# Three parts of a row table, a register load and a gather at other places of an expert stage

## The chip, the cores and the metric

The kernel runs on one core of a Trainium2 chip. The metric is the device time of one execution in microseconds (us): the median of the runs, beside one execution taken with the profiler. The engines are named as the profile names them: PE is TensorE, PEld its weight load, DVE VectorE, ACT ScalarE, POOL GpSimd, SP the engine that issues most DMAs. A name with a q (DVEq) is that engine's sequencer.

## What is computed

Three layers in a row: sigmoid attention, a mixture of experts in which each token goes to the one expert of its largest logit, and a gated feed-forward layer. Cut to its core:

```python
scores = q @ k.T / sqrt(64) - log(448)          # 4 batches, 12 heads, 448 tokens
x = sigmoid(scores) @ v                         # -> 1792 tokens x 768
xn, en = x / norm(x), expert_emb / norm(expert_emb)
logits = xn @ en.T / tau                        # 8 experts
idx, gate = argmax(logits), max(softmax(logits))
for e in range(8):
    m = idx == e
    out[m] = gate[m] * (relu(x[m] @ w1[e]) @ w2[e])   # 768 -> 1024 -> 768
y = (sigmoid(out @ w_gate) * (out @ w_val)) @ w_out   # 768 -> 1536 -> 768
```

All of it is float32; matrix products that need the precision are made as three products of a rounded part `hi` and a rest `lo`.

## The kernel before

**The expert stage.** Tokens are sorted by expert into tiles of 128 rows. `NSTAT` = 14 tiles are always computed, numbered p = 0 to 13; tiles past that are computed only if the data need them, in the body of an `If` (`tail_tiles`, line 1236; the branch is put down to line 1238), and with these data its body is skipped. Experts that leave only a few rows over get these rows in quarter tiles, the small tokens.

For each tile p: `gather(p)` fetches the rows from `xd` in DRAM by an indirect DMA that POOL issues; `front(p)` turns them on TensorE, ScalarE casts the result to `xh` (hi), and VectorE makes `xl` (lo) of it; four `h_chunk(p, c)` multiply by w1, ScalarE applies relu; `turn(p)` turns that and makes `hh` on ScalarE and `hl` on VectorE; four `y_chunk(p, c)` multiply by w2; `y_scale(p)` and `y_out(p)` scale by the gate and store the rows, by the row table `ridx`, to `yd`. The h chunks of tile p alternate with the y chunks of tile p - 1.

**Weights.** Each chunk of weights is loaded by SP into a raw buffer. `split_next()` makes the next chunk's `hi` on ScalarE (line 280) and its `lo` on VectorE (line 281) in a ring of four, and then issues the load that takes over the raw buffer. One `split_next()` follows each chunk of matmuls, so the splits of the w1 of tile 3 stand behind the h chunks of tile 2, and those of the w2 of tile 2 behind the h chunks of tile 3.

**Order.** The schedule is written out by hand: each engine works off its instructions in the order of the program, and semaphores hold an instruction until its inputs are there and its buffer is free. PSUM tiles come from `slot(...)`, four buffers taken in turn. Counted from there, `y_chunk(2, 0)` takes the buffer that the body of the `If` uses.

**The steps that the change touches.**
- `gate_b`, `gate_exp`, `gate_c`, `gate_d` make the gate weights; `gate_exp` is one exponential on ScalarE (line 873), for which a table is loaded; `gate_c` ends with products on POOL, `gate_d` has the small matmuls `psg` and ends with `gate_s` on VectorE (line 894).
- `turn(1)` (line 1773) is the turn of tile 1, called behind `gate_exp()`.
- `table_rows` (line 818) makes on VectorE the table of rows at which results are stored (`ridx`, `rowq`), and `rowb`. It is called once, behind the h chunks of tile 2 (line 1862).
- `n_tiles` (line 1869) loads the number of tiles from SBUF into a register of every engine; the `If` compares it.
- `front(3, later)` (line 1808) puts the making of `xl` of tile 3 off until behind the last h chunk of tile 2. `xl` has one buffer for all tiles.
- `small_ids` and `gather_small` (lines 811, 1159) make the list `idq` of the small tokens on VectorE and fetch their rows; `front_small` turns them on TensorE behind `turn(3)`.

```python
1808                front(3, later)
1811                later.pop()()
1813                turn(2)
1814                small_ids()
1815                gather_small()
1862            table_rows()
1869            n_tiles = nc.values_load(tabs["n"], min_val=0, max_val=NPAIR)
1870            tail_tiles(NSTAT)
```

Of the kernel before, what the change touches and what calls it, by code (L numbers as in the profile page):

```python
# [11 lines left out]
F32R = mybir.dt.float32r  # L12
# [10 lines left out]
D = H * HD  # L23
# [3 lines left out]
P = 128  # L27
# [10 lines left out]
NPAIR = N // P + E - 1  # L38
# [11 lines left out]
NW1 = KD * F1 // CH  # L50
# [99 lines left out]
def routed_kernel(ctx: ExitStack, tc: tile.TileContext, kqP, vP, emb, tau, w1P, w2P, wffP, cst, out):  # L150
    nc = tc.nc
# [53 lines left out]
    tabs = {}  # L205
# [609 lines left out]
        RED(out=rs, in_=r, axis=AX.X, op=ALU.add)  # L815
        V.tensor_copy(idq, rs)

    def table_rows():

        STT(out=tn, in0=tabs["ef"], scalar=-16.0, in1=tn, op0=ALU.mult, op1=ALU.add)  # L820
        have = per_tile(tabs["tot"], "rh")
        kept = per_tile(tabs["some"], "rs")
        for v in (have, kept):
            STT(out=v, in0=tn, scalar=float(-P), in1=v, op0=ALU.mult, op1=ALU.add)
            TT(out=v, in0=v, in1=once, op=ALU.mult)

        i = PAD
        for a, b in runs:
            TS(out=sums[:, 0, i : i + b - a], in0=kept[:, a:b], scalar1=0.0, scalar2=float(P), op0=ALU.max, op1=ALU.min)
            i += b - a  # L830
        for n, d in enumerate((1, 2, 4, 8, 16)):
            x = sums[:, n % 2]
            TT(out=sums[:, 1 - n % 2, PAD:], in0=x[:, PAD:], in1=x[:, PAD - d : PAD + NCOL - d], op=ALU.add)
        base = R("rb", [P, NCOL])
        i = PAD
        for a, b in runs:
            V.tensor_scalar_add(base[:, a:b], sums[:, 1, i - 1 : i - 1 + b - a], float(-N))
            i += b - a
        STT(out=rowb, in0=tn, scalar=float(-P), in1=base, op0=ALU.mult, op1=ALU.add)
        STT(out=rowb, in0=have, scalar=0.0, in1=rowb, op0=ALU.is_gt, op1=ALU.mult)  # L840
        big, few = slice(0, NPAIR), slice(NPAIR, NCOL)
        pt = [C("part").to_broadcast([P, NPAIR]), C("tq").to_broadcast([P, NQ])]
        for k, w in enumerate((big, few)):
            TT(out=have[:, w], in0=have[:, w], in1=pt[k], op=ALU.is_gt)
        TT(out=base, in0=base, in1=have, op=ALU.mult)
        V.tensor_scalar_add(base, base, float(N))
        ridx = cpool.tile([P, NPAIR], I32, name="ridx")
        rowq = cpool.tile([P, NQ], I32, name="rowq")
        for k, w in enumerate((big, few)):
            TT(out=base[:, w], in0=base[:, w], in1=pt[k], op=ALU.add)  # L850
        TT(out=base, in0=base, in1=own_row, op=ALU.subtract)
        TT(out=base, in0=base, in1=moves, op=ALU.mult)
        TT(out=base, in0=base, in1=own_row, op=ALU.add)
        V.tensor_copy(ridx, base[:, big])
        STT(out=rowq, in0=base[:, few], scalar=4.0, in1=C("jq").to_broadcast([P, NQ]), op0=ALU.mult, op1=ALU.add)
        tabs["r"], tabs["rq"] = ridx, rowq
# [11 lines left out]
    def gate_b():  # L868
        norm(ss, root, R("nt", [CP, NT]))
        TT(out=sh, in0=sh, in1=bc3(ss, E), op=ALU.mult)  # L870

    def gate_exp():
        A.activation(sh, sh, AF.Exp)
# [62 lines left out]
    def front(p, later=None):  # L936
        xg = xg_t.pop(p)
        ps = slot(f"xTp{p}")
        psf = ps.rearrange("p a b -> p (a b)")
        for k in range(KD):  # L940
            T.transpose(psf[:, k * P : (k + 1) * P], xg[:, k * P : (k + 1) * P], ident)  # L941
        if 0 <= p - 1 - PA < NA or p == PZ + 3:
            turn_small(min(p - 1 - PA, NA), psf[:, D : D + 256])
        hi = xp.tile([P, D], F32R, tag="xh", name=f"xh{p}")
        lo = xp.tile([P, D], F32R, tag="xl", name=f"xl{p}", bufs=1)
        A.copy(hi, psf[:, :D])
        xg_t["T", p] = (hi, lo)
        rest = lambda: V.tensor_sub(lo, psf[:, :D], hi)  # L948
        if later is None:
            rest()  # L950
        else:
            later.append(rest)
# [816 lines left out]
    gather(3)  # L1769
    y_chunk(0, 2, part[2])  # L1770
    gate_b()
    gate_exp()
    turn(1)
    y_chunk(0, 3, part[3])
    gate_c()
    for c in range(NW2):
        y_chunk(1, c, part[c])
        if c == 1:
            front(2)
            gate_d()  # L1780
            y_scale(0)
        split_next()
    own_rows()
    y_scale(1)
# [2 lines left out]
    for p in range(2, NSTAT):  # L1787
# [17 lines left out]
        for c in range(NW1):  # L1805
            h_chunk(p, c)
            if p == 2 and c == NW1 - 2:
                front(3, later)
                gather(5)
            elif p == 2 and c == NW1 - 1:  # L1810
                later.pop()()
            elif p == 3 and c == 0:
                turn(2)
                small_ids()
                gather_small()
            split_next()
            if c == 1 and p - PZ in (0, 1, 3):
                small_step((0, 2, 0, 6)[p - PZ])
            y = {(NSTAT - 2, 0): "T2", (NSTAT - 2, 2): "T4"}.get((p, c))
# [39 lines left out]
                    decode(DEC_ORDER[DEC_ATT + k], 2)  # L1859
            y_out(p - 1)  # L1860
        else:
            table_rows()
            y_out(0)
            y_out(1)
            tail = [buf("tail0", SB_Y, 6, 512, dt=F32R), buf("tail1", (SB_Y, 6 * 512), 4, 512, dt=F32R)]
            tail += [dp.tile([P, 6, 512], F32, tag="w64", name="tail_w"),
                     dp.tile([P, CH], F32, tag="w32", name="tail_x"), slot("tail")]
            tc.mark_branch_hint_location("beyond", hint='LikelyTaken', engines=[mybir.EngineType.PE])
            n_tiles = nc.values_load(tabs["n"], min_val=0, max_val=NPAIR)
            tail_tiles(NSTAT)  # L1870
        if 2 < p < NSTAT - 1:
            turn(p)
# [69 lines left out]
```

## Time and profile before

| | |
|---|---|
| median of three runs | 962.5 us (962.39 to 963.03) |
| the profiled execution | 966.3 us, of which 964.2 are the span from its first to its last instruction |
| TensorE busy | 932.3 us, 97% of the span |
| VectorE, ScalarE, POOL busy | 737.5, 544.6, 146.8 us |
| attention | 0 to about 157 us |
| expert stage | about 157 to 475 us; tiles 1 to 3, around which the change lies, 169 to 251 |
| feed-forward | about 475 us to the end |

A timeline gives the instructions of one engine in order, equal ones merged; the bracket behind one is the idle time of the engine before it and what released it. The windows give for each stretch how long an engine was busy and the share of full speed at which TensorE's clock was granted (1.00 is 2.4 GHz, 0.50 is 1.2 GHz). The times are those of the profiled execution.

### The profile page before, as it was taken

The page shows a single profiled execution, that of the slowest core. Times are in us where ns is not written, and L with a number is a line of the kernel's source. Part 1 is how long each engine was busy: PE and PEld are TensorE (multiplying, and loading weights), DVE is VectorE, ACT ScalarE, POOL GpSimd, SP SyncE. Part 2 cuts the span into 40 slices and gives each one's busy share as a digit, 9 for nine tenths or more (in the row PEclk, how much of TensorE's full clock was granted, in tenths as well). Part 3 has the DMA queues.
Part 4 walks back from the last instruction along what each step waited for, and adds up shares of the span by engine and source line. Part 5 has one row for each costly group of instructions (what it writes and reads, how often), then busy time and mean ns, then how long its engine had stood idle before and what let it go on. Part 6 is the DMA issues. An engine that isn't in the chain of part 4 may idle for free.

```text
span 964.2 us, 14875 instructions
## 1 busy us (share of the span) xinstructions
PE 932.3 (97%) x5757; PEld 784.3 (81%) x5757; DVE 737.5 (76%) x912; ACT 544.6 (56%) x645; POOL 146.8 (15%) x124
## 2 busy tenths in 40 slices
PE   9999999997999999999899999999998999999998
PEld 4555555886887788888788999989997999999998
DVE  6867767888899776799858888776896666658674
ACT  6586776575676676778644334446655434335551
POOL 0011113232062222224400000000220000000011
PEclk9999999998999999999889999999999999999999
DMA  8999867454699989766404564255131122125112
GB/s 306 334 327 344 319 215 267 163 167 155 259 401 417 345 323 334 261 262 201 148 1 163 196 196 164 82 203 206 66 132 44 55 66 66 66 99 197 50 50 82
DMA packets 36974, 186.40 MB, mean 193 GB/s; under 512 B 4680, under 2 KB 6744, under 8 KB 32800
## 3 DMA queue, kind: packets, MB, share of 16 engines
q1 hardware_dynamic: 25680, 134.29, 39.4%
q0 software_dynamic: 11216, 51.09, 14.1%
q8 instruction: 46, 0.75, 0.3%
q14 instruction: 32, 0.26, 0.1%
HBM read 180.94 MB, written 35.88 MB: 225 GB/s over the span
## 4 chain that ended last, share of the span: by engine, by line
PE 68%; DVE 3%; ACT 2%; DMA 2%; issue 1%; ACTq 0%; DVEq 0%; POOLq 0%
PE pb L1415 15%; PE pb L1414 15%; PE pb L1416 15%; PE h L1095 9%; PE y L1079 3%; PE y L1081 3%; PE y L1080 3%; PE qh L1184 2%; PE qy L1207 2%; DMA Y<-xd,idq 1%; PE hTp L1114 1%; DMA Y<-yd 1%; DVE rg L281 1%; PE xTp L941 1%; DVE tl L1577 1%
## 5 line engine op out<-in xcount | busy, mean ns | idle before, releaser
L281 DVE TENSOR_TENSOR rg<-raw,rg 128x1536 fp32r<-128x1536 f32 x104 | 180.2, 1757 | 36.9 <-ACT rg L280 32.6
L280 ACT CAST rg<-raw 128x1536 fp32r<-128x1536 f32 x102 | 150.2, 1480 | 64.8 <-PE y L1080 31.3
L1415 PE MATMUL pb<-yl,wh 128*128 128x448 f32 x288 | 106.8, 371 | 2.2 <-DVE yl L1350 2.2
L1095 PE MATMUL h<-rg,xh 128*128 128x512 f32 x336 | 103.6, 403 | 0.3 <-ACT rg L280 0.3
L1416 PE MATMUL pb<-th,sr 128*128 128x384 f32 x294 | 98.4, 335 | 1.4 <-DVE sr L1616 1.4
L1414 PE MATMUL pb<-th,sr 128*128 128x384 f32 x294 | 98.9, 337 | 0.0
L1415 PE MATMUL pb<-tl,sr 128*128 128x384 f32 x294 | 98.4, 335 | 0.2 <-DVE tl L1577 0.2
L436 ACT ACTIVATE attn<-sc,bias_s 128x896 f32<-128x896 f32 x84 | 79.2, 1003 | 28.6 <-PE sc L434 28.2
L1409 DVE TENSOR_TENSOR wl<-wr,wh 128x1536 fp32r<-128x1536 f32 (+1 forms) x43 | 68.0, 1581 | 17.9 <-ACT wh L1404 15.6
L1095 PEld LDWEIGHTS h<-rg,xh 128*128 128x128 f32 x336 | 62.0, 190 | 15.2 <-issue 1.6
L448 PE MATMUL av<-attn,v 128*64 128x448 f32 (+1 forms) x384 | 70.6, 545 | 0.3 <-DVE xT L453 0.2
L1079 PE MATMUL y<-rg,hh 128*128 128x384 f32 x192 | 67.5, 351 | 3.4 <-DVEq L1238 3.4
L1404 ACT CAST wh<-wr 128x1536 fp32r<-128x1536 f32 (+1 forms) x43 | 57.3, 1332 | 18.5 <-PE pb L1415 14.3
L1080 PE MATMUL y<-rg,hl 128*128 128x384 f32 x192 | 65.7, 342 | 1.4 <-DVE hl L1120 1.4
L1081 PE MATMUL y<-rg,hh 128*128 128x384 f32 x192 | 65.5, 341 | 1.5 <-DVE rg L281 1.5
L1095 PE MATMUL h<-rg,xl 128*128 128x512 f32 x168 | 61.9, 396 | 0.9 <-DVE xl L948 0.9
L1415 PEld LDWEIGHTS pb<-yl,wh 128*128 128x128 f32 x288 | 54.8, 190 | 7.3 <-DVE yl L1350 3.0
L1643 POOL DMA_INDIRECT out<-o,idc x12 | 17.5, 1460 | 271.5 <-ACT o L1661 227.6
L1416 PEld LDWEIGHTS pb<-th,sr 128*128 128x128 f32 x294 | 55.2, 188 | 1.7 <-DVE sr L1616 1.7
L1415 PEld LDWEIGHTS pb<-tl,sr 128*128 128x128 f32 x294 | 55.2, 188 | 0.6 <-DVE tl L1577 0.6
L1414 PEld LDWEIGHTS pb<-th,sr 128*128 128x128 f32 x294 | 55.2, 188 | 0.0
L1614 ACT CAST sr<-G 128x768 fp32r<-128x768 f32 x42 | 35.1, 839 | 30.4 <-PE pb L1415 18.5
(499 smaller groups left out, 2109.5 us busy)
## 6 DMA issues: line engine op xcount, KB each, us to landing
raw<-in_w1P SPq DMA_DIRECT2D x52, 768.0 KB
raw<-in_w2P SPq DMA_DIRECT2D x52, 768.0 KB
q<-wob SPq DMA_DIRECT2D x14, 1152.0 KB
wr<-wd SPq DMA_DIRECT2D x19, 768.0 KB
sg<-in_wffP SPq DMA_DIRECT2D x9, 1536.0 KB
kq<-in_kqP SPq DMA_DIRECT2D x24, 448.0 KB
stg<-in_wffP SPq DMA_DIRECT2D x5, 1536.0 KB
Y<-yd POOLq DMA_DIRECT2D x14, 384.0 KB, 6.3
```

The source lines that it names most:

```text
L280: (hi_eng.tensor_copy if hi_eng else A.copy)(hi, raw)
L281: V.tensor_sub(lo, raw, hi)
L436: A.activation(at_, ps[:, :, :S], AF.Sigmoid, bias=bias_s, scale=1.0 / math.sqrt(HD))
L448: T.matmul(av_t[j * HD : (j + 1) * HD, i % 2, :S], v[rows, j * HD : (j + 1) * HD], at_[rows, j, :], start=(u == first_unit(i)), stop=(u == ...
L1079: T.matmul(o, ah[:, ks], bh[:, w], start=(k == 0), stop=False)
L1080: T.matmul(o, al[:, ks], bh[:, w], start=False, stop=False)
L1081: T.matmul(o, ah[:, ks], bl[:, w], start=False, stop=(k == nk - 1))
L1095: T.matmul(ps[:, half, :], x[:, k * P : (k + 1) * P], w[:, s * 512 : (s + 1) * 512], start=(k == 0 and x is xh and w is hi), stop=(k == KD ...
L1409: V.tensor_sub(w_los(g, half), raw, w_his(sb, g, half))
L1414: T.matmul(o, ah[:, k], bh[:, k], start=(first and k == 0), stop=False, skip_group_check=open_)
L1415: T.matmul(o, ah[:, k], bl[:, k], start=False, stop=False, skip_group_check=open_)
L1416: T.matmul(o, al[:, k], bh[:, k], start=False, stop=(k == n - 1), skip_group_check=open_)
```

## The change

`table_rows` is cut into `rows_a`, `rows_b` and `rows_c`, with the same operations in the same order. `rows_a` and the load of `n_tiles` are called in the y chunks of tile 1, behind `gate_d` and `y_scale(0)`; `rows_b` behind the third h chunk of tile 2 and its split; `rows_c` where `table_rows` was, ahead of the `If`. `xl` of tile 3 gets a buffer of its own and is made at once behind its cast. `small_ids` and `gather_small` move from behind `turn(2)` to behind the last h chunk of tile 2, ahead of that chunk's split, of the row stores of tiles 0 and 1 and of the `If`. `turn(1)` is called ahead of `gate_exp`.

```diff
-    def table_rows():
+    tr = {}
+
+    def rows_a():
         STT(out=tn, in0=tabs["ef"], scalar=-16.0, in1=tn, op0=ALU.mult, op1=ALU.add)
         have = per_tile(tabs["tot"], "rh")
         kept = per_tile(tabs["some"], "rs")
         for v in (have, kept):
             STT(out=v, in0=tn, scalar=float(-P), in1=v, op0=ALU.mult, op1=ALU.add)
             TT(out=v, in0=v, in1=once, op=ALU.mult)
-
+        tr["have"], tr["kept"] = have, kept
+
+    def rows_b():
+        have, kept = tr["have"], tr["kept"]
         i = PAD
...
         STT(out=rowb, in0=have, scalar=0.0, in1=rowb, op0=ALU.is_gt, op1=ALU.mult)
+        tr["base"] = base
+
+    def rows_c():
+        have, base = tr["have"], tr["base"]
         big, few = slice(0, NPAIR), slice(NPAIR, NCOL)
...
-        lo = xp.tile([P, D], F32R, tag="xl", name=f"xl{p}", bufs=1)
+        lo = buf("xl3", SB_XA, D, dt=F32R) if p == 3 else xp.tile([P, D], F32R, tag="xl", name=f"xl{p}", bufs=1)
...
     gate_b()
+    turn(1)
     gate_exp()
-    turn(1)
     y_chunk(0, 3, part[3])
...
             front(2)
             gate_d()
             y_scale(0)
+            rows_a()
+            n_tiles = nc.values_load(tabs["n"], min_val=0, max_val=NPAIR)
         split_next()
...
             h_chunk(p, c)
             if p == 2 and c == NW1 - 2:
-                front(3, later)
+                front(3)
                 gather(5)
             elif p == 2 and c == NW1 - 1:
-                later.pop()()
+                small_ids()
+                gather_small()
             elif p == 3 and c == 0:
                 turn(2)
-                small_ids()
-                gather_small()
             split_next()
+            if p == 2 and c == NW1 - 2:
+                rows_b()
...
-            table_rows()
+            rows_c()
             y_out(0)
             y_out(1)
...
-            n_tiles = nc.values_load(tabs["n"], min_val=0, max_val=NPAIR)
             tail_tiles(NSTAT)
```

## Rows read from the trace of the kernel before

**Rows 1.** Windows: us, TensorE busy (instructions), granted clock, DMA share, GB/s.

```profile
209.38:212.79 3.41, 2.19 (x9) 1.00 0.69 262
224.20:231.00 6.80, 4.47 (x12) 0.50 0.14 59
241.30:244.70 3.40, 3.40 (x9) 0.50 1.01 381
246.00:460.00 214.00, 213.98 (x1561) 1.00 0.83 307
```

**Rows 2.** Timeline, TensorE: start, us, engine, line, operation [idle before <- releaser].

```profile
185.90 1.04 PE L1114 MATMUL hTp<-cs,hr 128*128 128x128 f32 x8
...
190.23 0.44 PE L1080 MATMUL y<-rg,hl 128*128 128x384 f32 x1 [0.82 <-DVE hl L1120]
...
194.41 0.81 PE L941 MATMUL xTp<-cs,xg 128*128 128x128 f32 x6
...
212.41 0.96 PE L1095 MATMUL h<-rg,xl 128*128 128x512 f32 x3 [0.92 <-DVE xl L948]
...
220.28 0.82 PE L941 MATMUL xTp<-cs,xg 128*128 128x128 f32 x6
224.51 0.66 PE L1079 MATMUL y<-rg,hh 128*128 128x384 f32 x1 [3.41 <-DVEq L1238]
...
227.87 0.69 PE L1081 MATMUL y<-rg,hh 128*128 128x384 f32 x1 [1.45 <-DVE rg L281]
...
239.82 1.33 PE L1172 MATMUL xTq<-cs,Y 128*128 128x128 f32 x12 [1.27 <-DMA Y<-xd,idq]
```

**Rows 3.** Timeline of VectorE, 188 to 225 us, same columns.

```profile
188.95 1.23 DVE L1120 TENSOR_TENSOR hl<-hTp,hh 128x1024 fp32r<-128x1024 f32 x1 [1.28 <-ACT hh L1117]
...
197.61 0.18 DVE L894 TENSOR_SCALAR gate_s<-gf 128x21 f32<-128x21 f32 x1
200.12 5.10 DVE L281 TENSOR_TENSOR rg<-raw,rg 128x1536 fp32r<-128x1536 f32 x3 [2.33 <-ACT rg L280]
...
209.73 1.76 DVE L281 TENSOR_TENSOR rg<-raw,rg 128x1536 fp32r<-128x1536 f32 x1 [1.10 <-ACT rg L280]
...
213.94 0.18 DVE L820 SCALAR_TENSOR_TENSOR tn<-ef,tn 128x26 f32<-128x26 f32 x1
...
216.29 0.44 DVE L829 TENSOR_SCALAR sums<-rs 128x7 f32<-128x7 f32 x5
...
218.79 0.26 DVE L844 TENSOR_TENSOR rh<-rh,cs 128x21 f32<-128x21 f32 x2
...
224.46 1.23 DVE L1120 TENSOR_TENSOR hl<-hTp,hh 128x1024 fp32r<-128x1024 f32 x1 [3.59 <-DVEq L1238]
```

**Rows 4.** Timeline of ScalarE: the exponential, the cast behind it, the other table load.

```profile
187.71 0.31 ACT L873 ACTIVATE sh<-sh 112x128 f32<-112x128 f32 x1 [4.68 <-DVE sh L870]
187.92 1.00 ACT L1117 CAST hh<-hTp 128x1024 fp32r<-128x1024 f32 x1
...
462.92 1.28 ACT L1119 ACT_TABLE_LOAD   x1
```

**Rows 5.** Timeline of POOL: gather of tile 2, gather of the small tokens.

```profile
186.02 1.02 POOL L932 DMA_INDIRECT xg<-xd,idx  x1 [14.93 <-DVE root L360]
...
230.47 1.54 POOL L1162 DMA_INDIRECT Y<-xd,idq  x1 [4.09 <-DMA raw<-in_w2P]
```

**Rows 6.** Issues of two gathers, us to landing last; landings of row stores.

```profile
xg<-xd,idx POOLq DMA_INDIRECT x1, 6.8
...
Y<-xd,idq POOLq DMA_INDIRECT x1, 9.2
...
DMA to landing us min/median/max: 3.0/7.7/14.4
```

**Rows 7.** Line 1869, VectorE's load of the number of tiles: ns, start us.

```profile
L1869 DVEq TENSOR_LOAD <-np_i x1: 543/543/543, 220.6 to 220.6; - x1
```

**Rows 8.** Waits of ScalarE, 240 to 480 us: total us, times, longest.

```profile
ACT rg L280 <- PE h L1095: 26.9, 22, 3.1
```

## Prediction, made before the changed kernel was run

> **What bounds the kernel now.** I read the busy time by stretch first [rows 1]: from 246 to 460 us, where nearly all experts are computed, TensorE is busy without a gap, at full clock. So whatever TensorE wins before 246 us should arrive at the end. The second view is TensorE's timeline ahead of that [rows 2], in which the bracket behind an instruction is its idle time and who ended it. The reader is to see six waits: 0.82 us for `hl` of tile 1; 0.92 for `xl` of tile 3; 3.41 before the first matmul of `y_chunk(2, 0)`, ended by VectorE's sequencer at line 1238, which is the branch of the `If` over the spare tiles; two more inside that chunk, until VectorE has made `hl` of tile 2 and the rest of the first w2 chunk (the last, 1.45, at 227.87); and 1.27 for the gathered small tokens. The clock by stretch [rows 1] adds to this: it is granted at half (1.2 GHz) from 224.2 to 231.0, behind the stretch in which TensorE stood, and again from 241.3 to 244.7, behind the wait for the small tokens.
>
> Why does `y_chunk(2, 0)` wait for VectorE's branch? Its PSUM slot is one of four taken in turn, and four slots earlier is the one that the body of the `If` uses. So it may start only when VectorE has passed the branch. VectorE's timeline [rows 3] shows why that is late: all of `table_rows` stands in the queue ahead of it, from 213.94 us on.
>
> So the bound from 197 to 228 us is VectorE's own queue. From the end of `gate_s` (197.61 + 0.18 = 197.79) to the matmul at 227.87 [rows 2, 3] are 30.08 us, with only three gaps: 2.33 and 1.10 us, both for a cast of ScalarE, and 3.59 us for the branch. The rest, 30.08 - 7.02 = 23.06 us, is work in order.
>
> **Part 1: `turn(1)` ahead of `gate_exp`.** Today ScalarE's cast `hh` of tile 1 starts at 187.92, behind the exponential [rows 4], though its transposes are done at 185.90 + 1.04 = 186.94 [rows 2]. Put first, it starts near 186.98, and all behind it, `hl` and the matmul at 190.23, comes 0.94 us earlier; TensorE's 0.82 us are gone. What is late next is the exponential. Its table load has to precede it, and the cast now precedes both. The nearest row is the other table load of this kernel: it starts without idle time behind a cast and takes 1.28 us [rows 4]. So the cast ends at 187.98, the load at 189.26 and the exponential, 0.31 us, by 189.6. `gate_c` waits today for `hl`, whose end is 188.95 + 1.23 = 190.18 [rows 3]; it still starts half a us earlier, and the later exponential is hidden. Gain 0.94 us, provided that the rows of gather(2) are there when TensorE turns them at 194.41 - 0.94 = 193.47: issued at 186.02 [rows 5], landed 6.8 us later [rows 6], that is 192.8.
>
> The Trainium skill ("ScalarE: Activation LUTs", section "What ACT_TABLE_LOAD costs") speaks against this step: it gives a switch of tables 2.66 us, of which 1.38 are a drain. The trace does not agree, there is no idle time ahead of the load in rows 4. By the page the exponential would end near 191.0, 0.8 us behind today's start of `gate_c`, and the step would bring nothing.
>
> **Part 2: `rows_a` in the gap.** Its nine operations take 216.29 - 213.94 = 2.35 us [rows 3]. They go behind `gate_s`, in front of the gap of 2.33 us. `gate_s` and the cast that ends the gap both shift by 0.94 us, so the cover stays.
>
> **Part 3: the load of `n_tiles`.** VectorE's takes 0.54 us at 220.6 [rows 7], and the branch can only follow it: 0.5 us go there. In its new place it lies half beside the end of `rows_a`; between 0.2 and 0.54 us, I take 0.4. On the other engines it is covered: TensorE and ScalarE have matmuls and `y_scale(0)` in work, on SP and POOL nobody waits. If TensorE's queue were empty there, 0.5 us.
>
> **Part 4: `xl` of tile 3 in its own buffer.** Today it must wait until tile 2's last matmuls have read the shared buffer, so it is issued behind the split at 209.73. Now it follows its cast and fills the gap of 1.10 us ahead of that split [rows 3]; TensorE's 0.92 us go. `rows_b` (218.79 - 216.29 = 2.50 us) and `small_ids` now stand ahead of the last split of tile 3's w1, which ends near 215.4 us instead of 213.94. `h_chunk(3, 3)` wants it near 216.2: its nine matmuls end at 220.28 today and take some 2.1 us, and the two waits ahead of it are gone. So 0.8 us of cover; beyond it, one for one.
>
> **Part 5: `rows_c` alone ahead of the branch.** No work leaves VectorE's queue between `gate_s` and the matmul of 227.87; it is packed. New length: 23.06 + 0.4 for the load + 3.1 for the branch (3.59 - 0.5) = 26.6 us, against 30.08. That is 3.5 us less, from a start 0.94 us earlier: the matmul comes 4.4 us earlier, at 223.4. TensorE, rid of 0.94 and 0.92 us, ends its turn of 220.28 near 219 and still stands some 2 us before the branch. VectorE stays the bound there, so TensorE's own waits must not be added to the 4.4.
>
> **Part 6: small tokens gathered earlier.** POOL starts that gather at 230.47 after 4.09 us of idle [rows 5], queued behind two row stores and the branch, and it lands 9.2 us after its start [rows 6]. Now it needs only `idq`, ready near 213.8, and stands ahead of the stores: landed by 224, wanted at 239.82 - 1.27 - 4.4 = 234.1. The two stores stand behind it for some 3 us of POOL, but their table is ready only near 217.4. TensorE's 1.27 us go.
>
> **Part 7: the clock.** From 241.3 to 244.7 nine matmuls were served at half clock [rows 1]; at 2.4 GHz the same take half of the 3.4 us, so up to 1.7 are lost, and I take 1.6. The stretch follows the wait that part 6 removes, so I let it go with it. The earlier one stays, as TensorE still stands most of the time from 219 to 223.4; how its end lies to the matmuls can change its price by -1.4 to +1 us, I take 0.
>
> **Sum:** 4.4 + 1.3 + 1.6 = 7.3 us. The profiled execution took 966.3 us, 964.2 of it span, and becomes 959.0. The median of the runs is 962.5, 3.8 less than the profiled one; with the same gain it becomes **955.2 us**.
>
> **The rivals.** (a) The second half-clock stretch stays though its wait is gone, as a sequel of the first. For it: 1.2 us of idle between 209.38 and 212.79 were followed by no fall [rows 1]; against it: nothing but the order of the rows. 962.5 - 5.7 = 956.8. (b) Both half-clock stretches go, 1.4 us more: 953.8. (c) The exponential comes late by a drain behind the cast (the page's rule above, as a mechanism here): `gate_c`, POOL's spread and `gate_s` fall back by 1 us, 956.2. (d) Weight loads swallow a part: they are issued as splits free their buffers, so earlier by what TensorE wins, into a DMA share of 1.01 [rows 1]. Against: from 240 to 480 us ScalarE's casts wait for TensorE, up to 3.1 us at a time, which is room that a later load would use first [rows 8]. Half lost is 958.9. (e) It is not the slot that holds `y_chunk(2, 0)`: then parts 2 to 5 bring nothing, 0.9 + 1.3 remain, 960.3. (f) Slower: the branch on VectorE costs its 3.1 us waiting for code, today beside little traffic. Moved to 217 to 221 us, it would run beside the small gather and a row store. The row for a slow transfer is the slowest row store, 14.4 us to land [rows 6]; a branch as slow costs 11.3 us more, 962.5 - 7.3 + 11.3 = 966.5. It decides from 7.3 us of delay on.
>
> **Chances.** Forecast 0.44, (a) 0.24, (b) 0.08, (c) 0.08, (d) 0.07, (e) 0.04, (f) 0.05. A difference of 0.2%, 1.9 us, is about what a measurement of this kernel tells from none. Faster by more: all but (f) and a fifth of (d) and half of (e), 0.92; within it 0.04; slower 0.04, as a small delay in (f) only cancels the gain. Forecast, (a), (b) and (c) hold 0.84 and lie between 953.8 and 956.8; with the bounds of the first half-clock stretch (down to 953.0 in what is likely) and (d) at half, the range is 953.0 to 959.0.
>
> **What the profile after would show.** Right: VectorE without a gap from `gate_s` to the branch; the first matmul of `y_chunk(2, 0)` near 220.7 us instead of 224.51, about 2 us of idle before it, still ended by VectorE's branch; no wait for `xl` of tile 3 and none for the small tokens; full clock after 240 us. Wrong: the matmuls of `gate_d` waiting for POOL near 194 us (c), casts waiting for loads after 246 (d), a branch well over 3.1 us (f), half clock after 235 (a), or `h_chunk(3, 3)` waiting for its split, which would mean that VectorE's queue is too full for part 4.

## The result and the profile after

| | before | changed |
|---|---|---|
| median of four runs | 962.8 us (962.4 to 964.9) | **957.0 us** (956.0 to 957.4) |
| the profiled execution, its span | 966.3, 964.2 us | 956.7, 954.6 us |
| TensorE busy | 932.3 us | 928.1 us |

The ratio is 0.9908, with a 95% interval of 0.9885 to 0.9931: faster, by 8.9 us of 962.8 (6.6 to 11.1). The medians of the table differ by 5.8 only, which is a ratio of 0.9940 and lies outside that interval. The kernel before varies more than its first four runs show: in the experiments below, 63 runs of it on three chips had medians of 966.1 to 967.6 us. So the ratios are what I go by.

The order of TensorE's instructions is the same in both kernels, so each matmul can be set against itself. The difference of the start times, after minus before, grows in steps, and each step has a place:

| place (us before) | step | sum |
|---|---|---|
| to 168.95: a gather of tile 1 landed earlier; the change does not reach that far ahead | -0.7 | -0.7 |
| 190.23: `hl` of tile 1 | -0.9 | -1.6 |
| 195.06: `psg` of `gate_d` | +1.3 | -0.3 |
| 227.87: third matmul of `y_chunk(2, 0)` | -3.6 | -3.9 |
| 239.82: the small tokens | -1.55 | -5.4 |
| 241 to 245: half clock | -1.55 | -7.0 |
| 374.88: results turned for the feed-forward | +1.0 | -6.0 |
| 477.75: first matmul of the feed-forward | -3.1 | -9.1 |
| 478 to 496: half clock in the kernel before | -3.4 | -12.5 |
| 497 to the end: a wait for `y0T4lo` (0.66 us) and half clock in the changed kernel | +2.9 | -9.6 |

TensorE's timeline after the change, the lines that answer to [rows 2]:

```profile
185.23 1.03 PE L1123 MATMUL hTp<-cs,hr 128*128 128x128 f32 x8
...
188.62 0.44 PE L1089 MATMUL y<-rg,hl 128*128 128x384 f32 x1
...
192.72 0.82 PE L950 MATMUL xTp<-cs,xg 128*128 128x128 f32 x6
194.78 0.75 PE L666 MATMUL psg<-spg,bm 112*128 112x78 f16 x16 [1.24 <-POOL spg L659]
...
209.54 1.63 PE L1104 MATMUL h<-rg,xh 128*128 128x512 f32 x6 [0.30 <-ACT rg L280]
...
218.81 0.82 PE L950 MATMUL xTp<-cs,xg 128*128 128x128 f32 x6
221.13 0.41 PE L1088 MATMUL y<-rg,hh 128*128 128x384 f32 x1 [1.50 <-DVEq L1247]
222.35 0.44 PE L1089 MATMUL y<-rg,hl 128*128 128x384 f32 x1 [0.81 <-DVE hl L1129]
224.02 0.69 PE L1090 MATMUL y<-rg,hh 128*128 128x384 f32 x1 [1.23 <-DVE rg L281]
...
234.41 1.31 PE L1181 MATMUL xTq<-cs,Y 128*128 128x128 f32 x12
```

The waits for `hl` of tile 1, `xl` of tile 3 and the small tokens are gone. The three at `y_chunk(2, 0)` have the same releasers as before, with 1.50, 0.81 and 1.23 us. A new one stands at 194.78: 1.24 us for a product on POOL.

VectorE's timeline after, the answer to [rows 3]:

```profile
196.22 0.18 DVE L903 TENSOR_SCALAR gate_s<-gf 128x21 f32<-128x21 f32 x1
...
199.10 5.10 DVE L281 TENSOR_TENSOR rg<-raw,rg 128x1536 fp32r<-128x1536 f32 x3 [0.48 <-ACT rg L280]
...
208.03 0.96 DVE L957 TENSOR_TENSOR xl<-xTp,xh 128x768 fp32r<-128x768 f32 x1 [0.27 <-ACT xh L955]
209.41 1.76 DVE L281 TENSOR_TENSOR rg<-raw,rg 128x1536 fp32r<-128x1536 f32 x1 [0.42 <-ACT rg L280]
...
221.07 1.22 DVE L1129 TENSOR_TENSOR hl<-hTp,hh 128x1024 fp32r<-128x1024 f32 x1 [3.17 <-DVEq L1247]
```

The gap of 2.33 us behind `gate_s` is down to 0.48, the one of 1.10 to 0.42, the branch's of 3.59 to 3.17.

ScalarE after, the answer to [rows 4]: the cast is first, and the table load and the exponential follow without a pause.

```profile
186.30 1.02 ACT L1126 CAST hh<-hTp 128x1024 fp32r<-128x1024 f32 x1 [5.28 <-PE hTp L1123]
187.33 1.28 ACT L882 ACT_TABLE_LOAD   x1
188.63 0.31 ACT L882 ACTIVATE sh<-sh 112x128 f32<-112x128 f32 x1
```

POOL after, the answer to [rows 5]: the gather of the small tokens is issued 16 us earlier, and TensorE's line at 234.41 has no wait.

```profile
214.26 2.27 POOL L1171 DMA_INDIRECT Y<-xd,idq  x1 [4.31 <-DVE idq L816]
```

Windows after, the answer to [rows 1]: the half-clock stretch at `y_chunk(2, 0)` lasts 3.4 us instead of 6.8, the second one is gone, and the experts behind it run as before (columns as in [rows 1], TensorE alone).

```profile
223.80:227.20 3.40, 3.18 (x10) 0.50 0.28 116
236.00:239.40 3.40, 3.40 (x15) 1.00 0.93 340
242.00:456.00 214.00, 213.15 (x1561) 1.00 0.83 307
```

The largest surprise is 230 us behind the change. TensorE's timeline, kernel before, at the first product of the feed-forward:

```profile
477.75 0.74 PE L1414 MATMUL pb<-y0B11hi,wh 128*128 128x448 f32 x1 [3.11 <-ACT yo L1141]
```

and the changed kernel, same matmul:

```profile
468.69 0.36 PE L1423 MATMUL pb<-y0B11hi,wh 128*128 128x448 f32 x1
```

Before, this matmul stood 3.11 us until ScalarE had read the result of the last tile, `y13`, out of PSUM; now it stands for nothing. The wait also has a sequel. The 6 us from this matmul on, kernel before:

```profile
477.70:483.70 6.00, 5.95 (x16) 0.50 0.16 66
```

and changed kernel:

```profile
468.60:474.60 6.00, 6.00 (x31) 1.00 0.25 104
```

TensorE's clock was granted at half behind the wait, and in full where the wait is gone. The changed kernel has a half-clock stretch of its own later, from 483 to 490 us; the last two rows of the table set the two against each other.

### The profile page after: what moved, and what is told of

The parts are those of the page before. It is cut to its first block, busy times and chain, and to the rows that moved or that the text cites. A ratio compares the mean times of both kernels' runs of the same rounds, so it can differ in the third digit from the quotient of the medians.

```text
span 954.6 us, 14878 instructions
## 1 busy us (share of the span) xinstructions
PE 928.1 (97%) x5757; PEld 781.6 (82%) x5757; DVE 737.4 (77%) x912; ACT 544.8 (57%) x645; POOL 147.9 (15%) x124
## 4 chain that ended last, share of the span: by engine, by line
PE 68%; DMA 2%; DVE 2%; ACT 2%; issue 1%; ACTq 0%; DVEq 0%
PE pb L1424 15%; PE pb L1425 15%; PE pb L1423 15%; PE h L1104 8%; PE y L1088 3%; PE y L1090 3%; PE y L1089 3%; DMA Y<-yd 2%; PE qh L1193 2%; PE qy L1216 1%; PE hTp L1123 1%; DMA yd<-yo,ridx 1%; PE xTp L950 1%; DVE tl L1586 1%; PE yTp L1313 1%
## 5 line engine op out<-in xcount | busy, mean ns | idle before, releaser
L281 DVE TENSOR_TENSOR rg<-raw,rg 128x1536 fp32r<-128x1536 f32 x104 | 179.9, 1752 | 32.0 <-ACT rg L280 26.6
```

The source lines that it names most:

```text
L281: V.tensor_sub(lo, raw, hi)
```

## The experiments

Each kernel was timed beside the kernel before. "us" is the ratio times 962.8, less 962.8. Where times of two traces are compared below, they are counted from the turn of tile 1's rows: it comes at another time in each execution (168.24 us in the changed kernel, 167.98 to 170.20 in the other traces), and no edit changes anything ahead of it.

| run | median us | ratio (95%) | us against before |
|---|---|---|---|
| changed kernel | 957.0 | 0.9908 (0.9885 to 0.9931) | -8.9 |
| e2_before_banks | 961.3 | 0.9946 (0.9926 to 0.9967) | -5.2 |
| e3_after_banks | 961.6 | 0.9950 (0.9930 to 0.9970) | -4.8 |
| e8_xl_late | 960.4 | 0.9942 (0.9914 to 0.9971) | -5.6 |
| e4_turn_back | 955.7 | 0.9897 (0.9869 to 0.9925) | -9.9 |
| e5_spread_dve | 957.0 | 0.9896 (0.9862 to 0.9931) | -10.0 |
| e9_gate_first | 956.0 | 0.9884 (0.9850 to 0.9919) | -11.2 |
| e6_small_late | 960.7 | 0.9934 (0.9908 to 0.9960) | -6.4 |
| e7_rows_together | 958.4 | 0.9914 (0.9887 to 0.9941) | -8.3 |
| e10_no_if | 952.6 | 0.9863 (0.9828 to 0.9897) | -13.2 |
| e11_if_c1 | 951.5 | 0.9861 (0.9831 to 0.9892) | -13.4 |
| e12_if_c0 | 950.7 | 0.9845 (0.9815 to 0.9874) | -14.9 |
| e13_before_if | 964.0 | 0.9967 (0.9946 to 0.9988) | -3.2 |

### The wait 230 us away: the order of PSUM banks

PSUM buffers are not dealt strictly in turn, though the text ahead of the prediction says so. As I read the program, each new tile gets the buffer that was released first in program order; no view of the profile shows bank numbers, so this rests on the three runs of this part and the next. `xl` of tile 3 is the last reader of its turned rows. Made earlier, it releases that buffer ahead of tile 2's relu, and two pairs of banks change places from there to the end: by that count `y13` lies in banks 0 and 1 before and in 2 and 3 after. The feed-forward's first product always goes to bank 0. Theory: this swap alone removes the 3.11 us. Two runs cross it: the kernel before with the feed-forward's banks permuted, and the changed kernel with the same permutation.

```diff
     one_bank += [pbp.tile([P, 512], F32, name=f"pb{i}") for i in range(8)]
+    one_bank[:] = [one_bank[i] for i in (2, 3, 0, 1, 4, 5, 6, 7)]
     gv_stage(0)
```

> The kernel before, with nothing but the eight PSUM banks of the feed-forward renamed, so that its first product does not take the bank in which y of tile 13 lies. Theory B (part of the gain comes from the far end of the expert stage, where TensorE waited 3.1 us for ScalarE to read y of tile 13): the wait near 475 us goes and the kernel is 2.5 to 4 us faster than before. Theory S (all of the 5.8 us was won before 250 us): within 0.5 us of before. Up to 470 us this is the kernel before once more: if the second half-clock stretch near 241 us belongs to it, it is there again.

> The changed kernel with the banks of the feed-forward renamed so that its first product does take the bank of y of tile 13, as in the kernel before. Theory B: the wait for ScalarE of some 3 us is back near 470 us and the time is 2.5 to 4 us above the changed kernel, 959.5 to 961. Theory S: 957 as the changed kernel.

Measured: the kernel before gains 5.2 us by that one line (3.2 to 7.1), more than the 2.5 to 4 that I expected; the changed one keeps 4.8 (2.9 to 6.7). The first matmul in TensorE's timeline, of e2_before_banks:

```profile
472.07 0.36 PE L1414 MATMUL pb<-y0B11hi,wh 128*128 128x448 f32 x1
```

and of e3_after_banks:

```profile
474.09 0.47 PE L1423 MATMUL pb<-y0B11hi,wh 128*128 128x448 f32 x1 [3.08 <-ACT yo L1150]
```

The wait goes and comes back with the bank, and half clock with it. The 6 us from that matmul on in e3_after_banks:

```profile
474.00:480.00 6.00, 5.91 (x21) 0.72 0.16 66
```

The four traces with this wait (the kernel before, e3_after_banks, e8_xl_late, e13_before_if) all show half clock right behind it, and the ten others full clock at the same matmuls. The 30 matmul intervals from there take 7.7 to 9.0 us in the four and 6.2 to 6.3 in the ten. So the bank costs 1.5 to 2.8 us beside the wait of 3.1, which covers the 5.2. The change's gain has two parts of about equal size, which nearly add up (5.2 + 4.8 against 8.9): the banks, whose order changes nothing that is computed, and the stage itself.

### `xl` of tile 3 at its old place, in its own buffer

```diff
             if p == 2 and c == NW1 - 2:
-                front(3)
+                front(3, later)
                 gather(5)
             elif p == 2 and c == NW1 - 1:
+                later.pop()()
                 small_ids()
```

> The changed kernel with xl of tile 3 made as late as before, but in its own buffer. Theory B, with the order of releases as cause: the PSUM bank of tile 3's turn is then released behind that of tile 2's h, the banks are dealt out as before, y of tile 13 lies in the feed-forward's first bank again and the 3 us wait is back: 959.5 to 961.5. Rival: the step is worth only its own wait, up to 0.9 us: 957 to 957.9.

Measured: 5.6 us below before, 3.3 above the changed kernel. TensorE's timeline of this run shows where it went and where it did not:

```profile
213.29 0.97 PE L1104 MATMUL h<-rg,xl 128*128 128x512 f32 x3 [3.29 <-DVE xl L957]
...
223.38 0.42 PE L1088 MATMUL y<-rg,hh 128*128 128x384 f32 x1
...
223.81 0.34 PE L1090 MATMUL y<-rg,hh 128*128 128x384 f32 x1
```

TensorE stands 3.29 us for `xl`, since `rows_b` stands ahead of it in VectorE's queue here, and then none of the three waits at `y_chunk(2, 0)` is left: the third matmul comes at 223.81, against 224.02 in the changed kernel. Behind its branch VectorE starts the split for that matmul at 221.77, so it is done near 223.5 here as well, and the earlier wait of TensorE has only taken the place of the later ones. This trace has its half clock at 214.2 to 217.6, in time that TensorE would have stood later anyway, and none at 224, so that at 246 us it is 1.8 us ahead of the changed kernel. What the run loses, it loses at 470 us: the first product waits 3.11 us for `y13` again, with half clock behind it. The early `xl` was worth its bank, and nothing in its own stage.

### `turn(1)` behind the exponential again

```diff
     gate_b()
-    turn(1)
     gate_exp()
+    turn(1)
```

> The changed kernel with turn(1) behind the exponential as before. Theory (what part 1 won, POOL gave back: its third product of the spread ran into VectorE's split and took 2.5 us instead of 0.9): TensorE waits 0.8 us for hl again, the small matmuls of gate_d wait no longer, the third product takes 0.9 us, and the time is within 0.4 us of the changed kernel, 956.6 to 957.4. Rival (the prediction's part 1): 0.9 us slower, 957.9.

Measured: 9.9 us below before, the changed kernel 8.9; the intervals overlap. TensorE's timeline of this run at `hl` of tile 1 and at the third matmul of `y_chunk(2, 0)`:

```profile
189.77 0.44 PE L1089 MATMUL y<-rg,hl 128*128 128x384 f32 x1 [0.82 <-DVE hl L1129]
...
223.76 0.69 PE L1090 MATMUL y<-rg,hh 128*128 128x384 f32 x1 [1.22 <-DVE rg L281]
```

Counted from the turn of tile 1 (168.51 us here), `hl` comes 0.9 us later than in the changed kernel, `psg` 0.4 earlier and the third matmul 0.5 earlier: the 0.9 us lost at `hl` are won back at `psg`, and more. The cause stands in the two timelines of POOL. Kernel before:

```profile
191.37 2.86 POOL L659 TENSOR_TENSOR spg<-am,g 112x416 f16<-112x416 f16 x3 [3.06 <-DVE g L882]
194.18 1.73 POOL L808 CAST own_row<-idx 128x21 f32<-128x21 int32 x1
```

Changed kernel:

```profile
190.25 4.47 POOL L659 TENSOR_TENSOR spg<-am,g 112x416 f16<-112x416 f16 x3 [2.66 <-DVE g L891]
194.68 0.20 POOL L808 CAST own_row<-idx 128x21 f32<-128x21 int32 x1
```

Of the changed kernel, the durations of the three products (ns, least, median and most):

```profile
L659 POOL TENSOR_TENSOR spg<-am,g x3: 880/885/2490, 190.3 to 192.2; 112x416 f16<-112x416 f16 x3
```

and VectorE's timeline at the third of them:

```profile
192.22 1.76 DVE L281 TENSOR_TENSOR rg<-raw,rg 128x1536 fp32r<-128x1536 f32 x1
```

The third product starts 0.02 us behind VectorE's split and takes 2.49 us instead of 0.885: it waits for the split. Before, it started first and had its 0.88; POOL's next instruction, the cast, fell beside the split and took 1.73 us instead of 0.20. The loser is whoever starts second. The Trainium skill ("SBUF — State Buffer", section "Who interferes with whom") has this rule: a VectorE instruction with two inputs in SBUF and a GpSimd instruction that reads SBUF contend for a port pair, and whoever issues first has it for the whole instruction. The trace agrees, with the prices above. With `turn(1)` first, the two start within 0.02 us of each other, so chance decides: in six traces POOL's product lost, in two (e8_xl_late and e12_if_c0) VectorE's split did, with 2.48 us instead of 1.76, and TensorE did not wait for POOL.

### The third product on VectorE, and `gate_d` ahead of `xl` of tile 2

```diff
-            eng.tensor_tensor(out=r[:, :, q, :], in0=am, in1=bc3(v, ncol), op=ALU.mult)
+            (V if name == "g" and q == 2 else eng).tensor_tensor(out=r[:, :, q, :], in0=am, in1=bc3(v, ncol), op=ALU.mult)
```

> The changed kernel, with one of the three products of the spread of gate_c put on VectorE in place of POOL. Theory A (what turn(1) gained was given back to POOL: its third product took 2.49 us beside VectorE's split where it took 0.88 before, and TensorE then stood 1.2 us for it): TensorE's wait of 1.2 us for that product goes, and gate_d's matmuls begin up to 1.2 us earlier than 194.8 us on the trace's scale. The time gains less, since VectorE's own queue sets the first matmul of y_chunk(2, 0) and now holds one product more: 0 to 1 us below the changed kernel. Rival (VectorE's split is what is late, on whichever engine the product stands): the product on VectorE waits behind the same split of 1.76 us, TensorE still stands over 1 us, and the time stays.

The second run adds this (and a permutation that keeps `y13` off the first product's bank):

```diff
-            front(2)
+            front(2, later)
             gate_d()
             y_scale(0)
+            later.pop()()
             rows_a()
```

> The changed kernel with the spread's third product on VectorE, and gate_d put ahead of the rest of tile 2 (xl), with the two PSUM bank pairs ordered so that the feed-forward's first product doesn't take the bank of y13, as in the changed kernel. Theory A (the path to y_chunk(2, 0) is VectorE's queue from gate_s on): gate_s starts about 1 us earlier, and the first matmul of y_chunk(2, 0) with it; 0.5 to 1 us below the changed kernel. Rival (what is won there is lost to xl of tile 2, which h_chunk(2, 0) waits for): the same time as the changed kernel, or up to 1 us more.

Measured: 957.0 and 956.0 us, 10.0 and 11.2 us below before: neither can be told from the changed kernel by its time. The third matmul of `y_chunk(2, 0)` in e5_spread_dve:

```profile
224.57 0.69 PE L1090 MATMUL y<-rg,hh 128*128 128x384 f32 x1 [0.98 <-DVE rg L281]
```

In e9_gate_first it comes at 224.56. The wait for POOL is gone in both. Counted from the turn of tile 1 (169.77 and 170.00 us in these two traces), `psg` comes 1.4 us earlier than in the changed kernel, and this matmul 1.0 and 1.2 us earlier: at this place theory A holds. But half clock lasts 6.8 us behind it in both traces, where the changed kernel's trace has 3.4, and at 246 us 0.0 and 0.5 us of the lead are left. In the second run `gate_s` comes 0.9 us earlier than in the first (196.75 and 197.42 us), and 0.2 of that are left at the matmul.

### The small tokens at their old place

```diff
             elif p == 2 and c == NW1 - 1:
-                small_ids()
-                gather_small()
             elif p == 3 and c == 0:
                 turn(2)
+                small_ids()
+                gather_small()
```

> The changed kernel with the small tokens' list and gather back in their old place, behind turn(2). Theory A (that move is worth the wait of 1.27 us that it removed): TensorE's wait for the small tokens is back, 1.0 to 1.6 us; the rest of the timeline stays, so 1 to 1.6 us above the changed kernel. Forecast's part 7 (the half-clock stretch at 241 to 245 us is a sequel of that wait): half clock is back behind it, 2.5 to 3 us above. Rival (the wait is taken up later, by the 1.0 us that the changed kernel gave back at yT of the parts near 369 us): under 0.5 us above.

Measured: 6.4 us below before, 2.5 above the changed kernel and 3.6 above e5_spread_dve, which was timed beside it. TensorE's timeline of this run:

```profile
236.87 0.85 PE L1181 MATMUL xTq<-cs,Y 128*128 128x128 f32 x6 [0.95 <-DMA Y<-xd,idq]
240.32 0.56 PE L1181 MATMUL xTq<-cs,Y 32*128 32x32 f32 x6 [2.61 <-DMA Y<-xd,idx]
```

The wait is 3.56 us, more than the 1.27 before, because TensorE is there earlier and the second of the two gathers is late as well. Half clock is back behind it, from 241.9 to 245.3 us, and costs 1.6.

### The table in one piece

```diff
-            rows_a()
-            n_tiles = nc.values_load(tabs["n"], min_val=0, max_val=NPAIR)
...
-                rows_b()
...
+            rows_a()
+            rows_b()
             rows_c()
...
+            n_tiles = nc.values_load(tabs["n"], min_val=0, max_val=NPAIR)
             tail_tiles(NSTAT)
```

> The changed kernel with the table of rows back in one piece ahead of the If, and the load of n_tiles there as before; xl of tile 3, the small tokens and turn(1) stay in their new places, and with them the new PSUM banks. Theory A (the three parts of the table fill gaps of VectorE's queue, which binds y_chunk(2, 0)): 2.35 + 2.5 us of work stand again ahead of the branch, the gap behind gate_s opens again, and y_chunk(2, 0) comes 2 to 3.5 us later than in the changed kernel; 2 to 3 us above it, and still some 5 us below the kernel before, by the banks. Rival (the pieces do not matter, all of the change's time comes from the banks and the small tokens): under 0.5 us above the changed kernel.

TensorE's timeline of this run at `y_chunk(2, 0)`:

```profile
224.26 0.66 PE L1088 MATMUL y<-rg,hh 128*128 128x384 f32 x1 [4.27 <-DVEq L1247]
225.48 0.69 PE L1089 MATMUL y<-rg,hl 128*128 128x384 f32 x1 [0.56 <-DVE hl L1129]
227.15 0.69 PE L1090 MATMUL y<-rg,hh 128*128 128x384 f32 x1 [0.98 <-DVE rg L281]
```

The matmuls come 3.1 us later than in the changed kernel by the clock of the trace, and 2.7 counted from the turn of tile 1 (168.68 us here), as theory A has it; the trace keeps 2.8 us up to 730 us. The time says less: 958.4 against 957.0 us by medians, 8.3 against 8.9 by ratios, and the intervals overlap. The place is shown; its worth in the time is not settled by these runs.

### What the branch costs, and where it costs nothing

```diff
-            tail_tiles(NSTAT)
```

> The changed kernel without the If over the spare tiles (the part that handles experts with more rows than the fixed tiles hold is left out; these data do not use it), banks ordered so that the feed-forward's first product doesn't take the bank of y13. It measures what the branch itself still costs. Theory A (after the change y_chunk(2, 0) still stands for VectorE's branch): the wait of 1.50 us ended by VectorE's branch is gone, VectorE's chain is some 3 us shorter, and TensorE is bound by the next wait in order, the cast of tile 3 or its own work: 2 to 3 us below the changed kernel. Rival (behind the branch y_chunk(2, 0) stands for the rest of the first w2 chunk or the rest of tile 2, that is for VectorE's work and not for its branch): under 0.5 us.

Measured: 13.2 us below before, 4.3 below the changed kernel (the banks are again ordered so that `y13` is not in the way of the first product). The wait for VectorE's branch is gone: the third matmul of `y_chunk(2, 0)` comes 3.3 us earlier. So is the half-clock stretch at 223.8, which adds 1.4. Then the same `If` was moved instead of left out, with the lines that make its buffers: behind the second h chunk of tile 3 (e11, `c == 1`), and behind the first (e12, shown here).

```diff
             if p == 2 and c == NW1 - 2:
                 rows_b()
+            elif p == 3 and c == 0:
...
+                tail_tiles(NSTAT)
```

> The changed kernel with the If over the spare tiles moved behind the second chunk of tile 3's first layer, so behind hl of tile 2 and two splits in VectorE's queue; the rest of the table and the first row stores stay, and y13 keeps the changed kernel's bank. Theory A (what is left at y_chunk(2, 0) is VectorE's branch, and VectorE has slots in hand behind it): y_chunk(2, 0) comes 2.5 to 3 us earlier, as in the kernel without the If, VectorE's splits lie 3.2 us later from 222 us on without TensorE waiting for them; 2 to 4 us below the changed kernel. Rival (VectorE, without a gap to 235 us, has no slack there): TensorE waits the 3 us for the splits of the second layer instead, behind 224 us; within 1 us of the changed kernel.

> As the run with the If behind tile 3's second chunk, but behind the first: hl of tile 2 and one split ahead of the branch in VectorE's queue. y_chunk(2, 0) needs both halves of the first w2 chunk, the split behind hl among them. Theory A (VectorE's branch in front of the splits is what TensorE stands for): if that first split is among what stands ahead of the branch, as good as the other, 2 to 4 us below the changed kernel; if not, the matmul of that split waits for the branch, and 0 to 1.5 us below. Rival (no slack behind): within 1 us of the changed kernel.

Measured: 951.5 and 950.7 us, 13.4 and 14.9 us below before; e12's interval, 0.9815 to 0.9874, lies below that of the changed kernel. Both gain more than the 2 to 4 us expected against the changed kernel, 4.5 and 6.0; in the traces the third matmul comes 3.3 and 4.4 us earlier, and 1.4 more come from half clock that stays away. e12's trace also had the luck at `psg` told above, e11's had not. VectorE's timeline of e12_if_c0 shows why:

```profile
217.00 1.22 DVE L1129 TENSOR_TENSOR hl<-hTp,hh 128x1024 fp32r<-128x1024 f32 x1
218.14 1.75 DVE L281 TENSOR_TENSOR rg<-raw,rg 128x1536 fp32r<-128x1536 f32 x1
220.10 5.10 DVE L281 TENSOR_TENSOR rg<-raw,rg 128x1536 fp32r<-128x1536 f32 x3 [0.21 <-DVEq L1247]
```

The gap is 0.21 us instead of 3.17. The sequencer's entries of its line (ns, start us), in e12_if_c0:

```profile
L1247 DVEq COMPARE_BRANCH  x1: 72/72/72, 216.9 to 216.9; - x1
L1247 DVEq EVENT_SEMAPHORE  x1: 21/21/21, 219.9 to 219.9; - x1
```

and in the changed kernel:

```profile
L1247 DVEq COMPARE_BRANCH  x1: 72/72/72, 217.7 to 217.7; - x1
L1247 DVEq EVENT_SEMAPHORE  x1: 21/21/21, 221.0 to 221.0; - x1
```

and the second of them in e11_if_c1, whose compare is at 219.1:

```profile
L1247 DVEq EVENT_SEMAPHORE  x1: 21/21/21, 223.6 to 223.6; - x1
```

From the compare to the next entry are 3.0, 3.3 and 4.5 us. In e12 and e11 the sequencer is ahead of its engine: `hl` and a split, 1.22 + 1.75 = 2.97 us of work, have been issued when it branches in e12, two splits in e11, and the engine works them off meanwhile. The entry behind the branch stands where that work ends (218.14 + 1.75 = 219.89 in e12), so these two runs do not tell how long the branch itself takes there; they tell that it is covered. In the changed kernel the last instructions ahead of the branch are the short steps of `rows_c`, and the engine runs dry. The move does a second thing: the buffers of the `If` are taken earlier, and `y_chunk(2, 0)` no longer holds for the branch (in e11 it begins at 220.48). No run separates the two, but the third matmul needs the split that stood behind the branch in VectorE's queue.

The last run moves nothing but the `If` in the kernel before, to e12's place.

> The kernel before, with nothing changed but the place of the If over the spare tiles: it stands behind tile 3's first chunk, turn(2) and the small tokens, so behind hl of tile 2 and the next split in VectorE's queue; the load of n_tiles stays in front of that hl. y13 keeps the bank that it has in the kernel before, so the wait for it ahead of the feed-forward stays. Theory A (the sequencer takes 3 us for the branch wherever it stands, and the 3 us are hidden if 3 us of issued work stand ahead of them in the engine): VectorE's gap at the branch falls from 3.59 us to under 1, y_chunk(2, 0) comes some 3 us earlier, 3 to 4.5 us below the kernel before. Theory B (the moved branch is cheap only because the changed kernel loads n_tiles long before): the gap stays near 3 us, the split behind it is late, and the time is within 1 us of the kernel before.

Measured: 3.2 us below before (1.2 to 5.2), at the lower end of theory A. VectorE's timeline of this run:

```profile
222.79 1.76 DVE L281 TENSOR_TENSOR rg<-raw,rg 128x1536 fp32r<-128x1536 f32 x1
226.38 5.10 DVE L281 TENSOR_TENSOR rg<-raw,rg 128x1536 fp32r<-128x1536 f32 x3 [1.83 <-DVEq L1238]
```

The branch takes its time here too: the compare is at 222.8, the next entry at 226.2, 1.7 us behind the end of the split. The time that theory B gives, within 1 us of before, lies outside the interval. With the 0.36 us at the load of `n_tiles`, 2.2 us are left of 3.59, more than the 1 us that I expected. The list of the small tokens stands there between `hl` and the split, three short steps that each wait for the one before, and the sequencer gets to its branch only when the split is starting. Cover is what has been issued at that moment, 1.76 us, not what stands in the text ahead of it.

## Why the prediction was right, and where it was not

The forecast was 955.2 us with 953.0 to 959.0, the measured median 957.0; the gain was put at 7.3 us and is 8.9 by ratio, 5.8 by the first medians. The stage, which is all that the forecast spoke of, gave about 5 us (4.8 in e3_after_banks) of the 7.3; the banks gave the rest. By the trace the stage is 3.1 us at `y_chunk(2, 0)`, 1.55 at the small tokens and 1.55 of clock, less 1.0 given back at 369 us. That the total came so near is in part luck: a stage worth less than forecast met a gain that was not forecast. The stage alone, 962.5 - 4.8 = 957.7, would still lie in the range.

**Part 1, `turn(1)`, 0.94 us.** The first half was right: 0.9 us at `hl`, and the table load had no drain ahead of it. The Trainium skill ("ScalarE: Activation LUTs", section "What ACT_TABLE_LOAD costs") puts 1.38 us of drain on each switch; the trace does not agree here either, the load stands within 0.02 us of the end of the cast and the exponential within 0.02 of the end of the load. The step that failed is "it still starts half a us earlier", as if the start of `gate_c` settled its end: its third product met VectorE's split and lost 1.6 us. What I named as the sign of rival (c), `gate_d` waiting for POOL near 194 us, is there, but with another cause. By e4_turn_back the part is worth nothing: the times cannot be told apart, and the trace without it has the third matmul 0.5 us earlier.

**Part 2, `rows_a`, and part 3, the load.** Right: `rows_a` lies from 196.31 to 198.6 in the old gap; the split behind it starts 0.48 us late where I took 0.4 for the load, and the branch's gap is 3.17 us where I took 3.1.

**Part 4, `xl` and `rows_b`.** The cover of 0.8 us held, `h_chunk(3, 3)` does not wait. But the early `xl` gains nothing at `y_chunk(2, 0)` (e8_xl_late); its effect is the order of the banks, which no step of mine looked at.

**Part 5, the chain of VectorE.** The mechanism was right, the size was off by 1 us. From the end of `gate_s` to the third matmul are 224.02 - 196.40 = 27.6 us, not 26.6. Mis-sized was "it is packed": 0.27 and 0.42 us of waits for ScalarE's casts remain, 0.7 in all, 0.2 us are in a slower `rows_c`, and the rest in the pair of splits and the load. And the start came only 0.7 us earlier by the change (1.39 less the 0.7 of the gather), where part 1 promised 0.94. So the matmul came 3.1 us earlier instead of 4.4. Rival (e) fell, since parts 2 to 5 did bring these 3.1 us. The releaser of the chunk's first matmul is the branch in both traces, and without the branch or with its cost hidden 4 to 6 us go. But the chunk's third matmul waits for VectorE's split, so it is VectorE's queue, the branch in it, that binds there, and not the slot alone.

**Part 6, the small tokens.** Right: 1.27 us were forecast, 1.55 came, and e6_small_late brings the wait back. Of this, 1.0 us were given back at 369 us, where TensorE now stands 0.8 us for results on their way from DRAM.

**Part 7, the clock.** Its size was right (1.55 against 1.6) and its cause is likely, not certain. Half clock from 241 on is seen in the profiled executions of the kernel before and of e6_small_late, which wait for the small tokens, and in none of the eleven in which that wait is gone or (e13_before_if) 0.24 us. But e2_before_banks, up to there the same program as the kernel before, has a wait of 1.5 us there and no half clock. So the wait doesn't bring it each time, and that the two profiled executions differ by the full 1.55 is in part luck. Rival (a) fell; so did (b), as the first stretch is shorter and not gone.

**The far step.** The sum ended at 246 us, since TensorE is without a gap from there to 460. Behind 460 it is not, and the row that shows it, 3.11 us for `y13`, was in the profile and in no step: my steps followed the order of the work and not which buffer each tile gets. Making `xl` early moved a release, and with it every later assignment; its own buffer alone does not (e8_xl_late has that buffer and the wait).

**Rivals (d) and (f)** fell: TensorE is busy for 213.15 of the 214 us from 242 to 456, and its one wait there is the 0.80 us for stored results; and the branch leaves a gap of 3.17 us.

## What to carry to other kernels

An edit that changes when a buffer is released can change which bank every later tile gets: compare the assignment of buffers of both kernels, and look for long waits at the seams of stages, where the price falls due. A branch that costs its engine 3 us is free if as much work has been issued ahead of it: put it behind the longest instructions, not behind a string of short ones that wait for each other. And where one engine's queue sets an end, a wait of another engine ahead of it may be only a later one moved forward: 3.29 us of it in e8_xl_late left nothing at the matmul behind. Last, count two traces from a common point: the turn of tile 1, ahead of every edit, differs by up to 2.2 us in these.

## What the runs showed of the hardware

- The branch of the `If` keeps VectorE's sequencer 2.9 to 3.7 us, from the compare of 0.07 us to the next entry, in the eleven traces in which the engine runs dry behind it (217.7 to 221.0 in the changed kernel, 222.8 to 226.2 in e13_before_if). The Trainium skill ("Runtime: NRT & Kernel Launch", section "Instruction fetch mechanics") says that a taken branch to code that is not yet there waits for a DMA. The trace agrees as far as it goes. The DMA view of the changed kernel, 217.7 to 221.0 us, has this among its queues (packets, MB, share of 16 engines):

```profile
q14 instruction: 2, 0.02, 1.2%
```

All thirteen traces with the `If` have a packet of this queue 1.0 to 1.6 us behind VectorE's compare. From 212.5 to 250 us the changed kernel has 6, and e10_no_if, without the `If`, none. Which engine a packet serves, the view does not say.
- VectorE and POOL shut each other out for a whole instruction: POOL's product took 2.49 us instead of 0.88, its cast 1.73 instead of 0.20, VectorE's split 2.48 instead of 1.76. Which of the two loses changes from execution to execution, with starts 0.02 us apart or less.
- In some executions the feed-forward's matmuls run 2% slower at full clock for a whole pass, some 2.3 us. One window (columns as in [rows 1], TensorE alone) of e3_after_banks:

```profile
520.00:620.00 100.00, 100.00 (x486) 1.00 0.51 170
```

and of the changed kernel:

```profile
520.00:620.00 100.00, 100.00 (x495) 1.00 0.47 155
```

486 matmuls against 495 in 100 us of the same pass. It is there in the first pass (e5_spread_dve, e6_small_late), in the second (e7_rows_together, e9_gate_first), in both (e3_after_banks) or in none (the nine others, the kernel before and the changed kernel among them), and no run tells its cause.
